# A retention + mixture-of-experts kernel: first loads issued from two queues, one weight quarter fetched and split later, the last result scaled by two engines

## Chip, cores and metric

The kernel runs on one core of a Trainium2 chip. The metric is the device time of one execution in microseconds (us). Several executions are timed, and their median is quoted.

## What is computed

The reference has two parts. The first is a linear attention with a decay for each head (batch 4, 8 heads, 768 positions, head size 64):

```python
for t in range(S):
    state = gamma[None, :, None, None] * state + np.einsum('bhd,bhe->bhde', k[:, :, t], v[:, :, t])
    y[:, :, t] = scale * np.einsum('bhd,bhde->bhe', q[:, :, t], state)
```

Its output, 3072 rows of 512 features, goes into a mixture of 8 experts. Each row is sent to the one expert with the largest logit:

```python
logits = x @ w_gate
expert_idx = np.argmax(logits, axis=1)
gate_w = probs[np.arange(N), expert_idx]
for e in range(E):
    mask = expert_idx == e
    h = np.maximum(x[mask] @ w1[e], 0.0)
    out[mask] = gate_w[mask, None] * (h @ w2[e])
```

## The kernel before, in words

The attention is done in 24 chunks of 128 positions, six for each batch entry. One chunk's inputs (q and k transposed, v and k as they are, 256 KB each) lie in one tile `qkv_t`, and five such tiles take turns (`AHEAD = 5`). `load(g)` (line 212) issues the transfer of chunk g on the queue of SyncE (SP); the first two chunks are loaded in halves, q and k first, then v and k. Of the last chunk of a batch entry the second k isn't loaded.

The order of the work is written out by hand; each engine executes its instructions in that order. The loop over chunks begins at line 440. Iteration g does, in this order: the scores of chunk g + 1 (`scores`, two PSUM tiles that VectorE multiplies by the mask M into `Sb`, line 239), `carry(g)` (the state's part of the output, line 266), `scale(g + 2)` (GpSimd weighs v into `vs`, line 225), one `split` if the table `SPLITS` names the iteration, the gate's logits in some iterations (line 310, their copy by ScalarE at line 312, transposes at line 321 and a reduction by VectorE at line 326), `update(g)` (the state, line 250, copied with a factor by ScalarE, line 255), `output(g)` (line 277, then VectorE's multiplication into `xT`, line 283), `rows(g - 1)` (transposes at line 291, ScalarE's copy at line 293), `load(g + 5)`, and a `fetch` if the table `fetches` names the iteration. Around chunk 1 the scores stand in other places (`LATE`). In the sixth chunk of a batch entry there is no `update`.

The weights of expert 0 are prepared during the attention. `fetch(0, part)` (line 124) loads one quarter of 1 MB into one of two tiles `raw`; `split(0, part, i, ...)` takes a quarter of that tile, rounds it with ScalarE into `whi` (line 132) and lets VectorE subtract that into `wlo` (line 133). `fetches` = {2: 0, 7: 1, 14: 2, 18: 3} says after which chunk each quarter is fetched, `SPLITS` in which iteration each of the 16 pieces is split (pieces 0 to 7 in iterations 6 to 13, pieces 8 to 13 in 18 to 23).

Ahead of the loop stand the first loads, the constants (`cs`, in two transfers, of which the first holds what M is built from; G; the gate's weights `wgs`; `us32`), `WARM = 16` matmuls on a tile of ones that give TensorE something to do until data arrive (line 416), and the building of M by VectorE (line 429).

After the attention the experts follow one another: hidden layer (line 786), relu and rounding (lines 791 and 792), output layer (lines 811 and 813). The last expert's result has three row blocks of 128, 128 and 104 rows. `put_rows` (line 721) has VectorE multiply each block in PSUM by the gate weight into `yo` (line 725), and GpSimd scatters its rows to the output (line 603).

Of the kernel before, what the change touches and what calls it, by code (L numbers as in the profile page):

```python
# [13 lines left out]
AF = mybir.ActivationFunctionType  # L14
ALU = mybir.AluOpType
# [5 lines left out]
P = 128  # L21
# [10 lines left out]
E1 = E - 1  # L32
E9 = E + 1
KD = DM // P
# [5 lines left out]
JMAX = -(-CMAX // 32)  # L40
IDS = 0x3FFF
FILLED = (160, 320)
WARM = 16
LATE = 0
FILL = (2, 2, 4, 2)
AHEAD = 5
# [2 lines left out]
GROUPS = ((0, 6), (6, 6), (12, 6), (18, 4), (22, 2))  # L49
SENDS = {**{g: (g - 8, g - 7) for g in range(8, 15)}, 15: (7, 9), 16: (9, 10), 17: (10, 12),  # L50
         **{g: (g - 8, g - 7) for g in range(20, 24)}}
SPLITS = {**{g: (g - 6,) for g in range(6, 14)}, **{g: (g - 10,) for g in range(18, 24)}}

OFF = {}
_n = 0
# [44 lines left out]
def retention_moe(ctx, tc, qkv, wg, wts, cst, gdec, ustr, out):  # L100
    nc = tc.nc
# [25 lines left out]
    def split(pos, part, i, engine, n=2):  # L127
        if i == 0:
            wparts[pos, part] = [wp.tile([P, 4, 512], F32R, name=n, tag="w", bufs=11) for n in ("whi", "wlo")]
        raw, (hi, lo) = raws[pos, part], wparts[pos, part]  # L130
        h = slice(n * i, n * i + n)
        nc.scalar.copy(out=hi[:, h], in_=raw[:, h])  # L132
        engine.tensor_tensor(out=lo[:, h], in0=raw[:, h], in1=hi[:, h].bitcast(F32), op=ALU.subtract)  # L133
# [52 lines left out]
    with ExitStack() as actx:  # L186
# [12 lines left out]
        G = flat[:, 0:NP * C].rearrange("p (n t) -> p n t", n=NP)  # L199
# [7 lines left out]
        qs, vss, Sbs, xTs, lgs, Ys = {}, {}, {}, {}, {}, {}  # L207
        state = {"half": 0, "low": 0}

        half = (slice(0, D), slice(D, P))  # L210

        def load(g, part=slice(0, 4)):
            if g not in qs:
                qs[g] = ld.tile([P, 4, DM], F32, name="qkv_t", tag="ld")
            nc.sync.dma_start(out=qs[g][:, part], in_=qkv[g][:, part])

        def turned(g, i):
            return qs[g][:, i].rearrange("a (p t) -> a p t", p=NP)

        def scale(g):  # L220
            c = g % CPB
            if c == CPB - 1:
                return
            vs = wk.tile([P, H, D], F32, name="vs", bufs=3)
            nc.gpsimd.tensor_tensor(  # L225
                out=vs, in0=qs[g][:, 2].rearrange("a (h d) -> a h d", d=D),
                in1=cv[:, c, :].unsqueeze(2).broadcast_to([P, H, D]), op=ALU.mult)
            vss[g] = vs.rearrange("a (n t) d -> a n (t d)", t=2)

        def scores(g):  # L230
            Sb = wk.tile([P, 2, NP, C], F32, name="Sb")
            q, kt = turned(g, 0), turned(g, 1)
            sps = [ps_s.tile([P, NP, C], F32, name="sp") for _ in range(2)]
            for p in range(NP):
                for r in range(2):
                    nc.tensor.matmul(out=sps[r][:, p, :], lhsT=kt[half[r], p, :], rhs=q[half[r], p, :],  # L236
                                     start=True, stop=True)
            for r in range(2):
                nc.vector.tensor_tensor(out=Sb[:, r], in0=sps[r], in1=M[:, r], op=ALU.mult)  # L239
            Sbs[g] = Sb  # L240
# [162 lines left out]
        def lows(n, engine):  # L403
            for f in range(state["low"], n):
                low(f, engine)
            state["low"] = n

        load(0, slice(0, 2))
        nc.sync.dma_start(out=cs[:, 0:NFIRST], in_=cst[:, 0:NFIRST])
        load(0, slice(2, 4))  # L410
        load(1, slice(0, 2))
        nc.sync.dma_start(out=G, in_=gdec)
        load(1, slice(2, 4))
        warm = ps_m.tile([P, 512], F32, name="warm", tag="mt")
        for i in range(WARM):
            nc.tensor.matmul(out=warm, lhsT=ones, rhs=ones.unsqueeze(1).broadcast_to([P, 4, P]),
# [3 lines left out]
        nc.vector.memset(wgs, 0.0)  # L420
        nc.vector.memset(zeros, 0.0)
        us32 = rawp.tile([P, P], F32, name="us32", tag="raw")
        nc.sync.dma_start(out=cs[:, NFIRST:], in_=cst[:, NFIRST:])
        nc.sync.dma_start(out=wgs[:, :, 0:E], in_=wg.rearrange("(k p) e -> p k e", p=P))
        for g in range(2, AHEAD):
            load(g)
        nc.sync.dma_start(out=us32, in_=ustr)
        for r in range(2):
            nc.vector.tensor_tensor(
                out=M[:, r], in0=causal.unsqueeze(1).broadcast_to([P, NP, C]), op=ALU.mult,  # L430
                in1=cv[:, 0].rearrange("a (n t) -> a t n", t=2)[:, r].unsqueeze(2).broadcast_to([P, NP, C]))
        scale(0)
        scores(0)
        scale(1)
        stages = []
        logits_at = {3: 0, **{2 * i + 2: i for i in range(1, NCH // 2 - 1)}}
        fetches = {2: 0, 7: 1, 14: 2, 18: 3}
        fills = {3: (slice(0, E9, E), slice(FILLED[0], EARLY)),
                 **{i + 3: (slice(2 * i - 1, min(2 * i + 1, E)), slice(FILLED[1], 32 * JMAX)) for i in range(1, 5)}}
        for g in range(NCH):  # L440
# [5 lines left out]
            if g + 2 < NCH:  # L446
                scale(g + 2)
            for i in SPLITS.get(g, ()):
                split(0, *divmod(i, 4), nc.vector, 1)
# [71 lines left out]
        for g in range(GROUPS[-1][0], NCH):  # L521
# [7 lines left out]
                                       op0=ALU.mult, op1=ALU.add)  # L529
# [64 lines left out]
def sliced(a):  # L594
    return a.rearrange("p (q k r) -> p k q r", q=4, k=KD)


def featured(a):
    return a.rearrange("p (k q r) -> p k q r", q=4, k=KD)


def scatter_rows(tc, out, index, rows, group="rows"):
    sc = tc.nc.gpsimd.indirect_dma_start(  # L603
        out=out, out_offset=bass.IndirectOffsetOnAxis(ap=index, axis=0),
        in_=rows, in_offset=None, bounds_check=out.shape[0] - 1, oob_is_err=False)
    tc.declare_no_dep(sc.ins, group=group, reason="every token has one slot: the scattered rows are disjoint")
    tc.add_to_no_dep_group(group, sc.ins)
# [68 lines left out]
def moe_main(ctx, tc, wparts, fetch, split, xhl1, xgs, load_x, load_meta, token_index, regions, beyond, limit, natural,  # L676
             overflow, out):
    nc = tc.nc
# [9 lines left out]
    widths = [[min(P, c - a) for a in range(0, c, P)] for c in CAPS]  # L688
# [32 lines left out]
    def put_rows(e, py, j):  # L721
        w = widths[e][j]
        index, weight = natural[e]
        yo = yp.tile([P, DM], F32, name="yo")
        nc.vector.tensor_scalar(out=sliced(yo[:w, :]), in0=featured(py[:w, :]), scalar1=weight[:w, j, 1:2],
                                scalar2=None, op0=ALU.mult)
        scatter_rows(tc, out, index[:w, j:j + 1], yo[:w, :])

    def turn(e, py, k):
# [13 lines left out]
    with tc.manual_schedule():  # L743
        for e in range(E):
# [52 lines left out]
            for k in range(steps):  # L797
# [4 lines left out]
                py = pys[k % 2]  # L802
                n = 0
                for f in range(KF):
                    whi, wlo = wparts[e, 2 + f // 4]
                    hh, hl = hs[f]
                    for a, x in ((whi, hh), (wlo, hh), (whi, hl)):
                        se = dict(start=(n == 0), stop=(n == 3 * KF - 1))
                        if e in natural:
                            w = widths[e][k]  # L810
# [5 lines left out]
                if e in natural:  # L816
                    put_rows(e, py, k)
                else:
                    turn(e, py, k)
# [147 lines left out]
```

## Time and profile before

| | |
|---|---|
| median of 3 runs | 408.57 us (408.56 to 409.14) |
| the profiled execution, its own time | 408.45 us |
| its span in the profile | 406.6 us |
| TensorE (PE) busy | 395.6 us, 97% |
| VectorE (DVE) busy | 251.8 us, 62% |
| ScalarE (ACT) busy | 154.0 us, 38% |
| GpSimd (POOL) busy | 157.6 us, 39% |
| moved by DMA | 81.48 MB, mean 200 GB/s |

The span is what the profiler saw; the execution's own time has 1.85 us around it. All times below are us from the start of the span. A matmul counts as busy until its modelled end, so a busy PE is not a PE at its peak; whether PE waited is told by the wait that stands behind an instruction, in brackets: how long the engine was idle before it, and what ended that. A wait for a DMA ends when the transfer has landed.

### The profile page before, as it was taken

What the parts mean: (1) busy time and instruction counts of PE and PEld (TensorE: products, weight loads), DVE (VectorE), ACT (ScalarE), POOL (GpSimd) and SP (SyncE); (2) the same over time, 40 slices, a digit from 0 to 9 for tenths busy, and PEclk for the clock granted to TensorE, in tenths of its full rate; (3) what the DMA queues carried; (4) which work ended last, traced back from release to release, by engine and by line L of the source; (5) the groups of instructions that cost most, each with busy time, mean ns of one, the idle gap of its engine ahead of it and who ended that gap; (6) DMA issues with size and microseconds to landing.
All of it is one profiled execution on the core that took longest, in us unless ns stands there. A gap on an engine that the chain in (4) does not pass through costs nothing. (4 is left out here: it accounts for less than half of the span.)

```text
span 406.6 us, 8299 instructions
## 1 busy us (share of the span) xinstructions
PE 395.6 (97%) x3279; PEld 359.6 (88%) x3279; DVE 251.8 (62%) x466; ACT 154.0 (38%) x306; POOL 157.6 (39%) x146
## 2 busy tenths in 40 slices
PE   8799989999999999999999999999999999999994
PEld 4678868787898989999999999999999999999972
DVE  3557778588664576574677396557829557675410
ACT  2243535355651543440453154235325324523200
POOL 1322183723780031000178048308704831850741
PEclk9999999999999999999999999999999999999999
DMA  8999999996439694555158335906733682530111
GB/s 278 414 350 381 407 406 345 350 409 193 160 137 231 200 252 148 195 161 144 42 207 225 112 129 183 272 5 235 216 123 123 220 229 61 192 137 2 49 52 45
DMA packets 31177, 81.48 MB, mean 200 GB/s; under 512 B 5146, under 2 KB 19614, under 8 KB 24736
## 3 DMA queue, kind: packets, MB, share of 16 engines
q1 hardware_dynamic: 26096, 68.24, 50.2%
q0 software_dynamic: 5040, 12.69, 8.8%
q8 instruction: 26, 0.43, 0.4%
q14 instruction: 15, 0.12, 0.1%
HBM read 65.50 MB, written 16.15 MB: 201 GB/s over the span
## 5 line engine op out<-in xcount | busy, mean ns | idle before, releaser
L603 POOL DMA_INDIRECT out<-Z,sidx x80 | 93.8, 1173 | 140.3 <-DVE Z L738 119.0
L133 DVE TENSOR_TENSOR wlo<-raw,whi 128x1024 fp32r<-128x1024 f32 (+1 forms) x72 | 82.1, 1142 | 16.4 <-ACT whi L132 16.1
L132 ACT CAST whi<-raw 128x1024 fp32r<-128x1024 f32 (+1 forms) x72 | 68.1, 949 | 3.0 <-DMA raw<-w 2.9
L791 ACT ACTIVATE hh<-ph 128x256 fp32r<-128x256 f32 (+7 forms) x64 | 31.5, 492 | 97.0 <-PE ph L786 96.5
L813 PE MATMUL py<-hl,whi 128*128 128x452 f32 (+5 forms) x192 | 66.9, 349 | 0.0
L813 PE MATMUL py<-hh,whi 128*128 128x452 f32 (+5 forms) x192 | 66.9, 348 | 0.0
L813 PE MATMUL py<-hh,wlo 128*128 128x452 f32 (+5 forms) x192 | 66.9, 348 | 0.0
L792 DVE SCALAR_TENSOR_TENSOR hl<-ph,hh 128x256 fp32r<-128x256 f32 (+7 forms) x64 | 35.6, 556 | 36.5 <-ACT hh L791 35.4
L786 PE MATMUL ph<-xh,wlo 128*128 128x452 f32 (+6 forms) x224 | 50.1, 345 | 0.0
L786 PE MATMUL ph<-xl,whi 128*128 128x452 f32 (+6 forms) x224 | 50.0, 345 | 0.0
L786 PE MATMUL ph<-xh,whi 128*128 128x452 f32 (+6 forms) x224 | 49.9, 345 | 0.0
L239 DVE TENSOR_TENSOR Sb<-sp,xgs 128x512 f32<-128x512 f32 x48 | 30.9, 685 | 17.7 <-PE sp L236 17.6
L786 PEld LDWEIGHTS ph<-xh,whi 128*128 128x128 f32 x224 | 40.7, 188 | 0.9
L786 PEld LDWEIGHTS ph<-xh,wlo 128*128 128x128 f32 x224 | 40.7, 188 | 0.7
L786 PEld LDWEIGHTS ph<-xl,whi 128*128 128x128 f32 x224 | 40.5, 188 | 0.7
L225 POOL TENSOR_TENSOR vs<-qkv_t,cs 128x512 f32<-128x512 f32 x20 | 20.9, 1045 | 44.2 <-DMA qkv_t<-qkv 38.8
L622 ACT CAST xh<-xt 128x512 fp32r<-128x512 f32 (+7 forms) x26 | 14.3, 555 | 60.7 <-DVE xt L613 60.7
L813 PEld LDWEIGHTS py<-hl,whi 128*128 128x128 f32 x192 | 36.1, 188 | 0.8
L813 PEld LDWEIGHTS py<-hh,wlo 128*128 128x128 f32 x192 | 36.1, 188 | 0.8
L813 PEld LDWEIGHTS py<-hh,whi 128*128 128x128 f32 x192 | 36.1, 188 | 0.7
L603 POOL DMA_INDIRECT xs_dram<-xn,KEY x24 | 24.8, 1033 | 22.2 <-DVE Sb L239 8.5
L733 DVE STREAM_TRANSPOSE Z<-py 128x416 f32<-128x416 f32 (+3 forms) x24 | 15.0, 627 | 27.3 <-PE py L813 27.2
(120 smaller groups left out, 530.9 us busy)
## 6 DMA issues: line engine op xcount, KB each, us to landing
raw<-w SPq DMA_DIRECT2D x32, 1024.0 KB, 5.2
qkv_t<-qkv SPq DMA_DIRECT2D x18, 1024.0 KB, 9.2
qkv_t<-qkv SPq DMA_DIRECT2D x4, 768.0 KB, 9.0
xgs<-xs_dram SPq DMA_DIRECT2D x12, 211.2 KB, 7.6
xs_dram<-xn SPq DMA_DIRECT2D x7, 325.0 KB, 9.9
qkv_t<-qkv SPq DMA_DIRECT2D x4, 512.0 KB, 4.8
xgs<-xs_dram SPq DMA_DIRECT2D x8, 195.0 KB, 7.0
out<-Z,sidx POOLq DMA_INDIRECT x80, 4.3
```

What stands on the lines that cost most here:

```text
L132: nc.scalar.copy(out=hi[:, h], in_=raw[:, h])
L133: engine.tensor_tensor(out=lo[:, h], in0=raw[:, h], in1=hi[:, h].bitcast(F32), op=ALU.subtract)
L225: nc.gpsimd.tensor_tensor(out=vs, in0=qs[g][:, 2].rearrange("a (h d) -> a h d", d=D), in1=cv[:, c, :].unsqueeze(2).broadcast_to([P, H, D]) ...
L239: nc.vector.tensor_tensor(out=Sb[:, r], in0=sps[r], in1=M[:, r], op=ALU.mult)
L603: sc = tc.nc.gpsimd.indirect_dma_start(out=out, out_offset=bass.IndirectOffsetOnAxis(ap=index, axis=0), in_=rows, in_offset=None, bounds_c ...
L622: nc.scalar.copy(out=xh[:, :, sl], in_=src)
L733: nc.vector.transpose(out=Zs[e][:, 0:nb, k, :], in_=py[:, 0:32 * nb].rearrange("p (j c) -> p j c", c=32))
L786: nc.tensor.matmul(out=ph[:, :cap], lhsT=wparts[e, f // 4][a][:, kd, fo:fo + P], rhs=x[:, kd, :cap], start=(n == 0), stop=(n == 3 * KD - 1))
L791: nc.scalar.activation(out=hh[:, :cap], in_=ph[:, :cap], func=AF.Relu)
L792: nc.vector.scalar_tensor_tensor(out=hl[:, :cap], in0=ph[:, :cap], scalar=0.0, in1=hh[:, :cap].bitcast(F32), op0=ALU.max, op1=ALU.subtract)
L813: nc.tensor.matmul(out=py[:, :cap], lhsT=a[:, f % 4, k * P:(k + 1) * P], rhs=x[:, :cap], **se)
```

## The change

Four things: the halves of the first two chunks are each loaded in two transfers of 64 partitions, one issued by SP and one by ScalarE, with the other early transfers in another order; the dummy matmuls go from 16 to 9 and chunk 0's `vs` is made by VectorE; the second weight quarter is fetched after chunk 9 instead of 7, and its four pieces are split in iterations 13 to 16 instead of 10 to 13; the last row block is scaled in two halves of 256 columns, one by VectorE and one by ScalarE.

```diff
-WARM = 16
+WARM = 9
...
-SPLITS = {**{g: (g - 6,) for g in range(6, 14)}, **{g: (g - 10,) for g in range(18, 24)}}
+SPLITS = {**{g: (g - 6,) for g in range(6, 10)}, **{g: (g - 9,) for g in range(13, 17)}, **{g: (g - 10,) for g in range(18, 24)}}
...
-        def load(g, part=slice(0, 4)):
+        def load(g, part=slice(0, 4), apart=False):
             if g not in qs:
                 qs[g] = ld.tile([P, 4, DM], F32, name="qkv_t", tag="ld")
-            nc.sync.dma_start(out=qs[g][:, part], in_=qkv[g][:, part])
+            for queue, rows in zip((nc.sync, nc.scalar), half) if apart else ((nc.sync, slice(0, P)),):
+                queue.dma_start(out=qs[g][rows, part], in_=qkv[g][rows, part])
...
-        def scale(g):
+        def scale(g, engine=nc.gpsimd):
...
-            nc.gpsimd.tensor_tensor(
+            engine.tensor_tensor(
...
-        load(0, slice(0, 2))
+        load(0, slice(0, 2), True)
         nc.sync.dma_start(out=cs[:, 0:NFIRST], in_=cst[:, 0:NFIRST])
-        load(0, slice(2, 4))
-        load(1, slice(0, 2))
-        nc.sync.dma_start(out=G, in_=gdec)
-        load(1, slice(2, 4))
+        load(0, slice(2, 4), True)
+        nc.scalar.dma_start(out=G, in_=gdec)
+        load(1, slice(0, 2), True)
+        load(1, slice(2, 4), True)
...
+        load(2)
         nc.sync.dma_start(out=cs[:, NFIRST:], in_=cst[:, NFIRST:])
+        load(3)
         nc.sync.dma_start(out=wgs[:, :, 0:E], in_=wg.rearrange("(k p) e -> p k e", p=P))
-        for g in range(2, AHEAD):
-            load(g)
         nc.sync.dma_start(out=us32, in_=ustr)
+        load(4)
...
-        scale(0)
+        scale(0, nc.vector)
...
-        fetches = {2: 0, 7: 1, 14: 2, 18: 3}
+        fetches = {2: 0, 9: 1, 14: 2, 18: 3}
...
-        nc.vector.tensor_scalar(out=sliced(yo[:w, :]), in0=featured(py[:w, :]), scalar1=weight[:w, j, 1:2],
-                                scalar2=None, op0=ALU.mult)
+        first = KD // 2 if e == E1 and j == len(widths[e]) - 1 else KD
+        to, turned, share = sliced(yo[:w, :]), featured(py[:w, :]), weight[:w, j, 1:2]
+        nc.vector.tensor_scalar(out=to[:, 0:first], in0=turned[:, 0:first], scalar1=share, scalar2=None, op0=ALU.mult)
+        if first < KD:
+            nc.scalar.activation(out=to[:, first:], in_=turned[:, first:], func=AF.Copy, scale=share)
```

What this does to the order of the instructions on an engine, at three places. A row is a line number, the operation, the tile written and the tiles read; in brackets stand the semaphores that it waits for. DMAHW0 to DMAHW7 are eight semaphores that the transfers issued by SP and ScalarE take in turn, so the ninth transfer of the program waits until the first has landed.

The first place is SP's queue at the start of the program, before and then with the change:

```order
L215 DMA qkv_t<-qkv 128x1024
L409 DMA cs<-cst 128x200
L215 DMA qkv_t<-qkv 128x1024 x2
L412 DMA xgs<-gdec 128x512
L215 DMA qkv_t<-qkv 128x1024
L423 DMA cs<-cst 128x373
L424 DMA xgs<-wg 128x4x8 [waits DVE_49]
L215 DMA qkv_t<-qkv 128x2048 [waits DMAHW0_49]
L215 DMA qkv_t<-qkv 128x2048 [waits DMAHW1_49]
L215 DMA qkv_t<-qkv 128x2048 [waits DMAHW2_49]
L427 DMA us_149<-ustr 128x128 [waits DMAHW3_49]
```

```order
L216 DMA qkv_t<-qkv 64x1024
L410 DMA cs<-cst 128x200
L216 DMA qkv_t<-qkv 64x1024 x2
L216 DMA qkv_t<-qkv 64x1024 [waits DMAHW0_49]
L216 DMA qkv_t<-qkv 128x2048 [waits DMAHW2_49]
L425 DMA cs<-cst 128x373 [waits DMAHW3_49]
L216 DMA qkv_t<-qkv 128x2048 [waits DMAHW4_49]
L427 DMA xgs<-wg 128x4x8 [waits DMAHW5_49,DVE_49]
L428 DMA us_146<-ustr 128x128 [waits DMAHW6_49]
L216 DMA qkv_t<-qkv 128x2048 [waits DMAHW7_49]
```

The rows of 128x2048 are chunks 2, 3 and 4. Chunk 2 now stands ahead of the second part of the constants and the gate's weights, chunk 3 ahead of the gate's weights, and chunk 4 behind `us32`; G is gone to ScalarE's queue. Chunk 2 now waits for a half of chunk 0's v (DMAHW2) where it waited for chunk 0's q and k.

The second place is ScalarE in iterations 10 and 11, the first that lose a split, before, and then in iterations 10 to 13 with the change:

```order
L132 CAST whi<-raw 128x512 [waits DMAHW6_49]
L312 COPY xgs<-L 128x256 [waits PE_49,Activation_49]
L255 ACTIVATE ub_118<-U,cs 128x64 [waits PE_49]
L255 ACTIVATE ub_118<-U,cs 128x64 x3
L293 COPY xn<-xp 128x4x128 [waits PE_49]
L132 CAST whi<-raw 128x512
```

```order
L313 COPY xgs<-L 128x256 [waits PE_49,Activation_49]
L256 ACTIVATE ub_118<-U,cs 128x64 [waits PE_49]
L256 ACTIVATE ub_118<-U,cs 128x64 x3
L294 COPY xn<-xp 128x4x128 [waits PE_49]
L294 COPY xn<-xp 128x4x128 [waits DMAHW4_49,DMAHW5_49,DMAHW3_49,DMAHW6_49,DMAHW1_49,DMAHW7_49,DMAHW0_49,PE_49]
L313 COPY xgs<-L 128x256 [waits PE_49,Activation_49]
L256 ACTIVATE ub_117<-U,cs 128x64 [waits PE_49]
L256 ACTIVATE ub_117<-U,cs 128x64 x3
L294 COPY xn<-xp 128x4x128 [waits PE_49]
L358 ACTIVATE ex<-sh 128x48 [waits DVE_49]
L132 CAST whi<-raw 128x512 [waits DMAHW4_49]
```

The rounding that waits for the fetched quarter stood ahead of iteration 10's copy of the logits; it is now behind the exponential that ends iteration 12.

The third place is the end of the program, VectorE's row and then ScalarE's and GpSimd's, with the change:

```order
L729 TENSOR_SCALAR yo<-py_2072,meta_2076 104x2x4x32 [waits DMASW4_49,DVE_49,PE_49]
```

```order
L731 ACTIVATE yo<-py_2072,meta_2076 104x2x4x32 [waits DMASW4_49,DMAHW6_49,DMASW2_49,DVE_49]
```

```order
L605 DMA out<-yo,sidx_2077 3072x512 [waits DMASW6_49,Activation_49]
```

Before there was one row of 104x4x4x32 on VectorE, and the scatter waited for VectorE. The product on ScalarE waits for VectorE and not for PE, though it reads what PE wrote; the scatter waits for ScalarE.

## Rows read from the trace of the kernel before

**Rows 1.** The page's head and the DMA line of its second part: the span, and the busy share of the DMA engines in 40 equal slices of it, in tenths.

```profile
span 406.6 us, 8299 instructions
...
DMA  8999999996439694555158335906733682530111
```

**Rows 2.** All waits of PE in the program, the two largest of those that lie behind the first instruction: who waited for whom, us in total, times, the longest.

```profile
PE sp L236 <- DMA qkv_t<-qkv: 2.1, 2, 1.2
...
PE Y L266 <- DVE lg L326: 0.9, 1, 0.9
```

**Rows 3.** The timeline of PE during the attention: start, duration, engine, line, operation, tiles, count, and in brackets the idle time before and its releaser. The rows of L236 are the scores with which iterations begin: those at 6.67 and 13.59 are chunks 0 and 2, that at 17.31 is chunk 3 and begins iteration 2; those at 25.64, 30.19 and 33.49 begin iterations 4, 5 and 6, those at 49.70, 54.63 and 58.90 iterations 10, 11 and 12.

```profile
1.08 5.66 PE L416 MATMUL warm<-ones 128*128 128x512 bf16 x16 [1.08 <-DVE ones L143]
6.67 1.16 PE L236 MATMUL sp<-qkv_t 64*128 64x128 f32 x16
...
13.59 1.16 PE L236 MATMUL sp<-qkv_t 64*128 64x128 f32 x16 [1.20 <-DMA qkv_t<-qkv]
...
17.31 1.16 PE L236 MATMUL sp<-qkv_t 64*128 64x128 f32 x16 [0.95 <-DMA qkv_t<-qkv]
...
25.64 1.16 PE L236 MATMUL sp<-qkv_t 64*128 64x128 f32 x16
...
30.19 1.16 PE L236 MATMUL sp<-qkv_t 64*128 64x128 f32 x16
...
33.49 1.16 PE L236 MATMUL sp<-qkv_t 64*128 64x128 f32 x16
...
49.70 1.16 PE L236 MATMUL sp<-qkv_t 64*128 64x128 f32 x16
...
54.63 1.16 PE L236 MATMUL sp<-qkv_t 64*128 64x128 f32 x16
56.69 0.67 PE L266 MATMUL Y<-qkv_t,ub 64*64 64x128 f32 x16 [0.90 <-DVE lg L326]
...
58.90 1.16 PE L236 MATMUL sp<-qkv_t 64*128 64x128 f32 x16
```

**Rows 4.** The timeline of ScalarE and VectorE around the second quarter: its first rounding, the copy of the logits behind it and the subtraction; and, in the last line, the rounding with which iteration 13 began.

```profile
53.32 0.62 ACT L132 CAST whi<-raw 128x512 fp32r<-128x512 f32 x1 [2.92 <-DMA raw<-w]
53.84 0.37 ACT L312 COPY xgs<-L 128x256 f32<-128x256 f32 x1
...
53.97 1.98 DVE L133 TENSOR_TENSOR wlo<-raw,whi 128x512 fp32r<-128x512 f32 x1 [1.79 <-ACT whi L132]
...
65.11 0.60 ACT L132 CAST whi<-raw 128x512 fp32r<-128x512 f32 x1
```

**Rows 5.** SP's timeline: the issue of the gate's weights, of the second quarter, and of chunks 13 and 14, ahead of which the quarter stood (SP's rows have the time it took to issue, not to land).

```profile
4.34 0.45 SPq L424 DMA_DIRECT2D xgs<-wg  x1
...
42.26 0.34 SPq L124 DMA_DIRECT2D raw<-w  x1
45.27 4.32 SPq L215 DMA_DIRECT2D qkv_t<-qkv  x2
```

**Rows 6.** The timeline of VectorE and GpSimd at the start: M, chunk 0's v and chunk 1's v weighed as they land, and chunk 0's masked scores.

```profile
5.16 1.29 DVE L429 TENSOR_TENSOR xgs<-cs 128x512 f32<-128x512 f32 x2 [3.06 <-DMA cs<-cst]
...
6.58 1.04 POOL L225 TENSOR_TENSOR vs<-qkv_t,cs 128x512 f32<-128x512 f32 x1 [6.11 <-DMA qkv_t<-qkv]
...
7.87 1.29 DVE L239 TENSOR_TENSOR Sb<-sp,xgs 128x512 f32<-128x512 f32 x2 [1.42 <-PE sp L236]
...
10.26 1.04 POOL L225 TENSOR_TENSOR vs<-qkv_t,cs 128x512 f32<-128x512 f32 x1 [2.64 <-DMA qkv_t<-qkv]
```

**Rows 7.** The page's part on DMA issues: the gate's weights, with the time from issue to landing.

```profile
xgs<-wg SPq DMA_DIRECT2D x1, 16.0 KB, 6.7
```

**Rows 8.** Stretches of half a microsecond at the start, and of two microseconds later: us, PE, PEld, DVE, ACT and POOL busy, PE's granted clock, the busy share of the DMA engines, GB/s.

```profile
1.50:2.00 0.50, 0.50 (x3) 0.22 (x2) 0.50 (x1) 0.50 (x1) 0.00 (x0) 1.00 0.36 98
2.00:2.50 0.50, 0.50 (x3) 0.20 (x2) 0.10 (x1) 0.23 (x2) 0.00 (x0) 1.00 0.50 164
...
11.00:11.50 0.50, 0.50 (x18) 0.39 (x16) 0.29 (x1) 0.00 (x0) 0.30 (x1) 1.00 1.02 426
...
70.00:72.00 2.00, 2.00 (x28) 1.66 (x26) 1.48 (x7) 1.33 (x5) 0.23 (x1) 1.00 0.67 242
72.00:74.00 2.00, 2.00 (x50) 1.71 (x50) 1.29 (x2) 0.14 (x1) 1.70 (x2) 1.00 0.81 311
```

**Rows 9.** The timeline of PE's weight loads at the end of the dummy matmuls, one load to each matmul.

```profile
4.90 0.15 PEld L416 LDWEIGHTS <-ones 128*128 128x128 bf16 x1 [0.28 <-issue]
...
5.29 0.96 PEld L416 LDWEIGHTS <-ones 128*128 128x128 bf16 x5 [0.24 <-issue]
```

**Rows 10.** The timeline at the end of the program: VectorE's last product and GpSimd's last scatter.

```profile
400.95 0.75 DVE L725 TENSOR_SCALAR yo<-py,meta 104x512 f32<-104x512 f32 x1 [4.81 <-PE py L811]
402.01 1.01 POOL L603 DMA_INDIRECT out<-yo,sidx  x1 [4.62 <-DVE yo L725]
```

**Rows 11.** Groups of instructions from 100 to 145 us, by shape, two that read 256 columns of PSUM: count, busy us, mean ns of one, idle before.

```profile
L792 DVE SCALAR_TENSOR_TENSOR hl<-ph,hh 128x256 fp32r<-128x256 f32 x8 | 3.4, 422 | 3.0 <-ACT hh L791 3.0
L649 ACT ACTIVATE rx<-ph 128x256 f32<-128x256 f32 x8 | 3.1, 383 | 5.1 <-PE ph L645 4.3 <-POOL hl L653 0.8
```

**Rows 12.** The timeline late in the attention: chunk 20 lands, which GpSimd waits for, and PE begins with its scores.

```profile
85.21 1.04 POOL L225 TENSOR_TENSOR vs<-qkv_t,cs 128x512 f32<-128x512 f32 x1 [3.22 <-DMA qkv_t<-qkv]
...
86.96 1.16 PE L236 MATMUL sp<-qkv_t 64*128 64x128 f32 x16
```

## The prediction

> **What bounds the kernel now.** I first read PE's row of waits, because PE is busy for nearly the whole span of 406.6 us [rows 1]. Behind its first instruction the list has only two waits of weight: 2.1 us in two pieces for `qkv_t`, that is, for input chunks to land, and 0.9 us once for VectorE [rows 2]. So the kernel goes at PE's pace, and what can be gained lies at those waits, at PE's own work, and at the tail behind PE's last matmul.
>
> The timeline of PE says where the waits are: 1.20 us ahead of chunk 2's scores at 13.59, 0.95 us ahead of chunk 3's at 17.31, and 0.90 us in iteration 11 at 56.69 [rows 3]. From 17.31 on PE runs without a wait for data to iteration 10. So whatever moves the row at 17.31 moves everything behind it, and what shortens PE's way ahead of that row only makes it wait longer there.
>
> The DMA engines are the second thing to look at: through the first quarter of the span their share is nearly full [rows 1]. PE and DMA are close to each other in the attention, so a PE that runs ahead may find its chunks not landed. That is taken up below.
>
> The sum is made against the profiled execution, 408.45 us, which is 0.12 under the median of 408.57; I add that back at the end.
>
> **The second quarter, fetched and split later.** Iteration 10 lasts 54.63 - 49.70 = 4.93 us. Iteration 4 has the same place in its batch entry and the same work on PE, and lasts 30.19 - 25.64 = 4.55. Iteration 11 lasts 58.90 - 54.63 = 4.27, iteration 5 with the same work 33.49 - 30.19 = 3.30 [rows 3]. So 0.38 + 0.97 = 1.35 us are lost there. The reason is a queue: the quarter's transfer is issued at 42.26 [rows 5] and ScalarE stands for 2.92 us until 53.32 for it, with the copy of the logits behind it (53.84); VectorE begins its subtraction at 53.97 and takes 1.98 [rows 4], and what stands behind that on VectorE is the reduction that PE's row at 56.69 waits for. The change has no split in iterations 10 to 12, and ScalarE's copy of the logits there waits for PE alone. I take the whole 1.35.
>
> Does the wait come back in iteration 13? The fetch now stands behind chunk 14's transfer, issued by 49.6 [rows 5]; with the 53.32 - 42.26 = 11.1 us that the quarter took before it lands at about 60.7, less what PE gains. The rounding of iteration 13 ran at 65.11 [rows 4], behind iteration 12's exponential, and will be some 1.9 earlier, at 63.2. So 2.5 us are in hand; the transfer would have to take 13.6 us. The pieces themselves are 0.6 us of ScalarE [rows 4] and about 0.65 of VectorE (M's two products over 512 columns take 1.29 [rows 6]) in iterations of 3.3 to 4.6 us; up to 1.98 on VectorE has been seen [rows 4]. I cost them at nothing, hidden behind PE. Chunks 13 and 14 lose a megabyte ahead of them, which costs nothing either.
>
> **The start.** What counts is when chunk 3 lands. Two things change that.
>
> Order: ahead of chunk 3 only the gate's weights go away; the second part of the constants still stands between chunks 2 and 3. Chunk 1's v landed at 10.26 [rows 6], the gate's weights at 4.34 + 6.7 = 11.04 [rows 5, 7]. Of these 0.78 us the constants (128 x 373 x 4 B = 0.19 MB) need 0.45 at the 426 GB/s of a full stretch [rows 8]. That leaves 0.33 for the weights, the gain by order.
>
> Two queues: from 1.5 to 2.5 us the DMA engines are at 0.36 and 0.50 of their time [rows 8]; 0.57 us are idle. If that is SP's issuing, a second queue gives up to 0.57; if it is the latency of a first transfer, nothing; a loss of as much as the order brings, 0.33, is conceivable, since halves on two queues interleave and chunk 0 may land later. I take the middle of nothing and 0.57, about 0.3. Together 0.6: chunk 3 at 16.7.
>
> [...]
>
> The upper end: from chunk 2 to chunk 3 3.72 us pass (13.59 to 17.31, [rows 3]), where a chunk's 1.05 MB needs 2.46 at 426 GB/s. If the 1.26 us between are not lost again, the start gives 0.6 + 1.26 = 1.86.
>
> PE is no bound before that. Without its two waits it would reach chunk 3 at 17.31 - 1.20 - 0.95 = 15.16 [rows 3]. Now the dummy matmuls, 0.15 + 0.28 = 0.43 us apart [rows 9], end at 1.08 + 9 x 0.43 = 4.95, and the scores begin there, not at 6.67. But VectorE then builds M until 6.45, weighs chunk 0's v when it has landed (6.58) in about 0.65, and begins with the masked scores at 7.25 rather than 7.87 [rows 6]. So PE's way gets 0.6 shorter, to about 14.5, some 2.2 ahead of chunk 3. The fewer dummies and VectorE's product are thus costed at nothing; the wait for chunk 3 covers them. SP's issue of chunk 2 now waits for half of chunk 0's v, at about 6.6; then chunk 1 and G, 1.3 MB or 3 us of DMA work, are still ahead of it, so no gap opens.
>
> **The end.** The two halves are not at once: by the order ScalarE's product waits for VectorE's. VectorE's half takes 0.42 and ScalarE's 0.38 [rows 11], the handover 0.03 (53.94 to 53.97, [rows 4]): 0.83 in place of 0.75 [rows 10]. I take 0.1 longer. At once it would be 0.42, 0.33 shorter; and with a ScalarE that takes 0.62, as for 512 columns [rows 4], 0.3 longer.
>
> [...]
>
> **Does it stay gained?** Chunk 20 lands at 85.21 and is wanted at 86.96 [rows 12], 1.75 us in hand, and PE will come 1.95 earlier. But its transfer is issued when PE frees a buffer and so moves too, and the DMA engines had idle time in front of it: 0.66 and 0.38 us from 70 to 74 [rows 8]. So it can land 1.04 earlier, and 0.8 stay in hand. If it didn't move at all, 0.2 would be given back. Behind the attention no wait of PE is listed that reaches 0.9 [rows 2].
>
> **Sum:** -1.35 - 0.6 + 0.1 = -1.85; 408.45 becomes 406.6, and against the median **406.7 us**. Its own range is 406.3 to 407.1.
>
> **The rivals.**
> - *The queues bring nothing.* The start gives 0.33 by order or less: 408.57 - 1.35 - 0.33 + 0.1 = 407.0, with nothing at all from the start 407.3. For it: half the early idle may be latency. Chance 0.20. [...]
> - *Chunk 3 comes without its delay.* 408.57 - 1.35 - 1.86 + 0.1 = 405.5. For it: the delay between chunks 2 and 3 has no cause in the order of transfers; against: the same engines and nearly the same bytes. Chance 0.15.
> - *The stall moves.* The quarter lands after 63.2 or VectorE is too full in iterations 13 to 16, and 1.35 come back: 408.57 - 0.6 + 0.1 = 408.1. Against: 2.5 us in hand. Chance 0.12.
> - *Slower: PE stays at its lower clock.* [...] Chance 0.04.
>
> **How the numbers follow.** The forecast has 0.46, 0.03 are left to other things. 0.2% is 0.82 us, about what a measurement can tell from no change, so the line is at 407.75. The forecast and the first two rivals lie below it, 0.81, with a little of the rest: 0.82 faster. The moved stall lies within 0.2%: 0.13 with what is left. Slower: 0.05. The range takes in the first two rivals with the ends of their unknowns, 405.2 to 407.6; it leaves out the moved stall and the lower clock, and a start or end worse than any bound.
>
> **What would show it.** Right: chunk 3's scores at 16.4 to 17.0 and still with a wait for `qkv_t` ahead of them; iterations 10 and 11 at about 4.55 and 3.30 with no wait of ScalarE for `raw`; ScalarE's last product beginning when VectorE's ends. Wrong: a wait of PE for VectorE or of ScalarE for `raw` in iterations 13 to 16; waits for `qkv_t` at chunks 20 or 21; scores of 2.3 us in the first 15 us; the scatter at the end earlier, against PE's last matmul, than now.

## The result: 411.62 us, slower by 0.6%, and the profile after

The changed kernel takes 411.62 us (median of 6 runs, 410.29 to 412.01), the kernel before, beside it, 408.85 (6 runs, 408.56 to 409.83). The ratio is 1.0059, 95% interval 1.0041 to 1.0077: 2.4 us slower, where 406.7 was forecast. The profiled execution has 410.98, its span is 2.5 longer than in [rows 1].

From the page of the changed kernel, its span and the clock granted to PE in 40 slices of about 10 us:

```profile
span 409.1 us, 8294 instructions
...
PEclk9799999999999999999999999999999999999999
```

The timeline of PE in the changed kernel answers to [rows 3]. The rows at 5.03, 13.74, 17.88 and 20.98 are the scores of chunks 0 to 3, those at 53.37, 57.93 and 61.23 begin iterations 10, 11 and 12:

```profile
1.08 4.02 PE L417 MATMUL warm<-ones 128*128 128x512 bf16 x9 [1.08 <-DVE ones L143]
5.03 1.72 PE L237 MATMUL sp<-qkv_t 64*128 64x128 f32 x16
10.99 1.12 PE L251 MATMUL U<-vs,qkv_t 128*64 128x64 f32 x16 [4.24 <-DVE vs L226]
...
13.74 2.29 PE L237 MATMUL sp<-qkv_t 64*128 64x128 f32 x16
...
17.88 1.16 PE L237 MATMUL sp<-qkv_t 64*128 64x128 f32 x16 [0.50 <-DMA qkv_t<-qkv]
...
20.98 1.16 PE L237 MATMUL sp<-qkv_t 64*128 64x128 f32 x16 [0.33 <-DVE xT L284]
...
53.37 1.16 PE L237 MATMUL sp<-qkv_t 64*128 64x128 f32 x16
...
57.93 1.16 PE L237 MATMUL sp<-qkv_t 64*128 64x128 f32 x16
...
61.23 1.16 PE L237 MATMUL sp<-qkv_t 64*128 64x128 f32 x16
```

Three differences to [rows 3] make the whole result. Chunk 3's scores begin at 20.98 and not at 17.31: 3.67 us lost before anything else happens, and iteration 10 begins those 3.67 later (53.37, 49.70). Iterations 10 and 11 then last 4.56 and 3.30 instead of 4.93 and 4.27, so at iteration 12 the loss is 2.33. The last is at the end of the program. In time order, PE's last matmul and what follows, the answer to [rows 10]:

```profile
402.82 0.40 PE L816 MATMUL py<-whi,hl 128*104 128x512 f32 x1
403.26 0.48 DVE L729 TENSOR_SCALAR yo<-py,meta 104x256 f32<-104x256 f32 x1 [4.81 <-PE py L816]
403.78 0.47 ACT L731 ACTIVATE yo<-py,meta 104x256 f32<-104x256 f32 x1 [16.73 <-DVE yo L729]
404.56 1.02 POOL L605 DMA_INDIRECT out<-yo,sidx  x1 [4.86 <-DVEq L592]
```

PE's last matmul in the kernel before:

```profile
400.51 0.40 PE L811 MATMUL py<-whi,hl 128*104 128x512 f32 x1
```

The product on ScalarE begins where VectorE's ends. From the start of PE's last matmul to the scatter 1.74 us pass, where it was 1.50 (400.51 to 402.01 in the kernel before). So 3.67 - 1.34 + 0.24 = 2.57, less 0.02 between iteration 12 and PE's last matmul (2.31 later than before): the 2.5 of the span. What is to be explained is the start.

Stretches of five microseconds at the start, changed kernel, columns as in [rows 8]:

```profile
5.00:10.00 5.00, 1.75 (x17) 1.40 (x16) 1.29 (x2) 1.44 (x2) 0.00 (x0) 0.88 1.00 240
10.00:15.00 5.00, 4.01 (x40) 3.62 (x42) 2.58 (x4) 0.93 (x4) 0.00 (x0) 0.50 1.04 253
15.00:20.00 5.00, 4.44 (x77) 3.67 (x74) 2.25 (x4) 0.93 (x4) 2.09 (x2) 0.94 1.06 394
```

The same stretches of the kernel before:

```profile
5.00:10.00 5.00, 4.68 (x56) 2.88 (x54) 2.58 (x4) 0.93 (x4) 1.04 (x1) 1.00 1.01 371
10.00:15.00 5.00, 3.80 (x72) 3.26 (x72) 2.23 (x4) 0.93 (x4) 2.08 (x2) 1.00 1.04 422
```

The last two columns tell it: the DMA engines are as busy as before (1.00 and 1.04 of their time) and move 240 and 253 GB/s instead of 371 and 422. They aren't idle and don't wait for an issue; each byte takes them longer. Until about 15 us, while the halves are in flight, 10 us at some 150 GB/s less are 1.5 MB, or 3.5 us at 426. A share of 1.04 stood beside 253 GB/s here and beside 422 before, so the share alone doesn't tell the rate. PE's clock (third column from the end) falls to 0.50 behind PE's wait of 4.24 for chunk 0's v, and the scores at 13.74 take 2.29, where those at 17.88, with the clock back at 1.00, take 1.16.

### The profile page after: what moved, and what is told of

Read it like the earlier page. It is cut to its first block, busy times and chain, and to the rows that moved or that the text cites. A ratio compares the mean times of both kernels' runs of the same rounds, so it can differ in the third digit from the quotient of the medians.

```text
span 409.1 us, 8294 instructions
## 1 busy us (share of the span) xinstructions
PE 396.3 (97%) x3272; PEld 361.4 (88%) x3272; DVE 252.1 (62%) x467; ACT 154.8 (38%) x307; POOL 156.3 (38%) x145
## 3 DMA queue, kind: packets, MB, share of 16 engines
q0 software_dynamic: 5040, 12.69, 8.7%
## 5 line engine op out<-in xcount | busy, mean ns | idle before, releaser
L226 POOL TENSOR_TENSOR vs<-qkv_t,cs 128x512 f32<-128x512 f32 x19 | 19.9, 1047 | 47.7 <-DMA qkv_t<-qkv 38.9
```

The costliest lines, as they stand in the source:

```text
L226: engine.tensor_tensor(out=vs, in0=qs[g][:, 2].rearrange("a (h d) -> a h d", d=D), in1=cv[:, c, :].unsqueeze(2).broadcast_to([P, H, D]), o ...
```

## Experiments

Four readings of the slow start. **A**: a transfer into 64 adjoining partitions costs the DMA engines more time for each byte, by whichever queue. **B**: two queues at once hinder each other. **C**: PE's lower clock makes the start late. **D**: the new order of loads, where chunk 2's issue waits for a half of chunk 0's v. The runs were taken later, in sessions in which the kernel before itself had a median of 416.75 to 418.26 us, with a wait of PE of 2.7 to 4.2 us around 110 us in every trace, and behind it another 302 to 308 us that don't follow what was changed at the start (300 in the traces of the kernel before and of the changed kernel, which are from the first session). Totals are therefore given as ratios to the kernel before beside them, and the argument goes by the first 20 us of the traces. In these sessions the kernels with the old loads had chunk 3's scores at 17.54 to 18.25, so a few tenths between two single traces mean nothing.

### Is it the halves, the queues or the clock?

**Both halves on SP.**

```diff
-zip((nc.sync, nc.scalar), half)
+zip((nc.sync, nc.sync), half)
```

> The changed kernel with both halves of each early load issued by SP; ScalarE's queue keeps G alone. Theory A (a transfer into 64 adjoining partitions keeps the DMA engines busy longer for its bytes, whatever the queue): still slow, chunk 0's v lands at 9 to 12 us, the DMA engines move about 240 GB/s at a full share until chunks 0 and 1 are in, about 411 us or more. Theory B (two queues at work on the same engines slow each other): chunk 0's v lands at 6.5 to 7, about 400 GB/s from 5 us on, 407.0 to 407.8 us.

Ratio 1.0054 (1.0009 to 1.0099). Its stretch from 5 to 10 us:

```profile
5.00:10.00 5.00, 2.02 (x22) 1.63 (x24) 2.41 (x4) 0.00 (x0) 0.00 (x0) 0.81 1.06 238
```

Chunk 3's scores begin at 20.50 behind a wait of 1.83 for their data. One queue is as slow as two (238 and 240 GB/s).

**Two queues that carry whole tensors** of 128 partitions (SP q and v, ScalarE k and the second k).

```diff
+pieces = [(nc.sync, slice(part.start, part.start + 1)), (nc.scalar, slice(part.start + 1, part.stop))]
```

> The changed kernel with each early load divided by tensor instead of by partition: SP loads q and v, ScalarE k and the second k, all 128 partitions in each transfer. As many transfers, queues and semaphores as in the changed kernel. Theory A: fast, chunk 0's v at 6.5 to 7.2 us, 407.0 to 407.8 us. Theory B: slow as the changed kernel, v at about 10 us, about 411 us.

Ratio 0.9944 (0.9904 to 0.9983). Its stretch from 5 to 10 us:

```profile
5.00:10.00 5.00, 3.21 (x41) 2.67 (x42) 3.18 (x5) 2.29 (x6) 0.00 (x0) 0.98 1.04 381
```

From 10 to 15 us it moves 410 GB/s; chunk 3's scores begin at 17.21 without a wait for data. B is out.

**Even and odd partitions** in place of the lower and upper half, again 64 rows on each queue.

```diff
-zip((nc.sync, nc.scalar), half)
+zip((nc.sync, nc.scalar), (slice(0, P, 2), slice(1, P, 2)))
```

> The changed kernel with the halves taken as even and odd partitions: still 64 partitions to a transfer, two queues, the same sizes and order, but each transfer reaches over all 128. Theory A in its form that adjoining partitions are the trouble: fast, v at 6.5 to 7.2 us, 407.0 to 407.8 us. Theory A in the form that 64 rows to a transfer are the trouble, and theory B: slow, v at about 10 us, about 411 us.

Ratio 1.0021 (0.9977 to 1.0064), 367 GB/s from 5 to 10 us, chunk 3's scores at 18.13 without a wait for data. ScalarE's queue from 4.5 to 14 us (packets, MB, share of 16 engines' time), first in the changed kernel:

```profile
q10 hardware_dynamic: 387, 1.05, 48.3%
```

and with even and odd partitions:

```profile
q10 hardware_dynamic: 390, 1.04, 28.8%
```

Nearly the same packets and bytes take 1.7 times as long when the 64 rows adjoin. Neither the number of rows nor of packets nor of queues differs.

**PE kept busy** by twenty more dummy matmuls behind chunk 0's scores.

```diff
         scores(0)
+        for i in range(20):
+            nc.tensor.matmul(out=warm, lhsT=ones, ...)
```

> The changed kernel with 20 more dummy matmuls behind chunk 0's scores, so that PE is busy while it waits for chunk 0's v. Theory C (the lower clock of PE from 8.7 to 15.6 us, after its wait of 4.2 us, is what makes the start late): PE runs at its higher clock from 6 us on, chunk 3's scores come 1 to 3 us earlier than 20.98 and the time falls to 408.5 to 410.5 us. Theories A and B: the clock rises but chunk 3's scores stay at 20.5 to 21.1, since the chunk lands at 20.8, and the time stays within 0.5 us of 411.4.

Ratio 1.0070 (1.0022 to 1.0118). The stretches:

```profile
5.00:10.00 5.00, 4.35 (x30) 2.46 (x31) 1.60 (x3) 1.46 (x2) 0.00 (x0) 1.00 1.01 223
10.00:15.00 5.00, 4.78 (x70) 3.38 (x68) 2.94 (x6) 0.93 (x4) 0.00 (x0) 1.00 1.06 228
```

The clock is at 1.00 up to 15 us and the rate no better; chunk 3's v is at hand at 21.88 and its scores begin at 21.91. The lower clock is a consequence, not the cause.

**The halves alone** in the kernel before, the rest as it was.

```diff
-load(0, slice(0, 2))
+load(0, slice(0, 2), True)
...
```

> The kernel before with nothing but its first two chunks' halves each loaded as two transfers of 64 adjoining partitions, one by SP and one by ScalarE. Theory A: 230 to 250 GB/s at a full share of the DMA engines from 5 to 13 us, chunk 3's scores 3 to 4 us later than the kernel before, at 20.3 to 21.3, ratio about 1.008 to 1.009. If the change's other order of loads has a part in its loss (rival D: chunk 2's issue behind a half of chunk 0's v): chunk 3's scores at 17.3 to 18.5, ratio 1.000 to 1.003.

Ratio 1.0108 (1.0047 to 1.0169). 255 GB/s from 5 to 10 us; chunk 3 lands at 21.07, and its scores, with PE's clock at 0.50 from 17.5 to 20 us, begin at 22.42, later than expected. Without the new order chunk 3 comes as late (20.84 in the changed kernel), so D is out too.

**Another cut**: ScalarE's queue carries partitions 32 to 95, again 64 adjoining rows, SP's the outer two times 32.

```diff
+pieces = [(nc.sync, slice(0, 32)), (nc.sync, slice(96, P)), (nc.scalar, slice(32, 96))]
```

> The change with the rows of each early load cut in another way: ScalarE's queue carries partitions 32 to 95, again 64 adjoining rows in one transfer, SP's the outer 0 to 31 and 96 to 127. It tells apart two readings of theory A. If 64 adjoining rows as such are slow, ScalarE's queue needs as long for its 1.05 MB from 4.5 to 14 us as in the changed kernel (48% of the 16 engines' time there), and the rate stays at 230 to 250 GB/s. If what counts is which partitions are reached, ScalarE's queue needs 28 to 36% for them, and the rate from 5 to 12.5 us is 280 to 380 GB/s, between the halves and the interleaved rows; chunk 3's scores at 18 to 19.5 us. [...]

Its stretch from 5 to 10 us:

```profile
5.00:10.00 5.00, 1.67 (x17) 1.45 (x16) 1.29 (x2) 0.37 (x2) 0.00 (x0) 0.95 1.01 296
```

and ScalarE's queue from 4.5 to 14 us:

```profile
q10 hardware_dynamic: 329, 0.84, 29.6%
```

29.6% of 16 engines' 9.5 us for 0.84 MB are 54 us of an engine for each MB; the changed kernel has 70 and the even and odd rows 42 by the same division. So 64 adjoining rows as such aren't the cause: moved by 32 they are served faster. What each cut changes is both the partitions that a transfer writes and the rows of the chip's memory that it reads, and no run separates the two. Chunk 3's scores at 19.85 are later than expected: its data had landed by 17.52, and PE's clock was 0.50 from 10 to 15 us. The ratio, 1.0119 (1.0073 to 1.0165), is more than a start 1.1 us ahead of the changed kernel's would give; that rest isn't explained.

From 5 to 10 us the rates are 223 to 255 GB/s with halves, 367 with even and odd rows and 296 with the third cut. What in the way of the bytes makes them so isn't shown.

### The other parts of the start

**Whole loads, else as changed** (nine dummies, new order, G on ScalarE's queue), and **the same with sixteen dummies and the last product undivided**.

```diff
-zip((nc.sync, nc.scalar), half) if apart else ((nc.sync, slice(0, P)),)
+((nc.sync, slice(0, P)),)
```

```diff
-WARM = 9
+WARM = 16
...
-first = KD // 2 if e == E1 and j == len(widths[e]) - 1 else KD
+first = KD
```

> The change with every early load as one transfer of 128 partitions on SP; everything else of the change stays. Theory A (a transfer into 64 adjoining partitions costs the rate): the DMA engines move 370 to 420 GB/s from 5 to 15 us, chunk 0's v is weighed at about 6.6 to 7.2, chunk 3's scores begin at 16.8 to 17.5, and against the kernel before the whole is -1.35 (second quarter) + 0.24 (tail) - 0 to 0.5 (start) = -1.1 to -1.6 us, a ratio of about 0.9965. Rival C' (what is left of the change at the start, nine dummy matmuls, the other order, VectorE's product, is slow by itself, through the lower clock): chunk 3's scores at 19 or later though its data lie there, ratio 1.000 or more.

> The same with each early load as one transfer of 128 partitions on SP (G alone on ScalarE's queue). It prices the second queue where no half is involved. Theory A: the queue is worth little, chunk 3's scores within 0.3 us of the kernel with tensors on two queues, 16.5 to 17.0 us, ratio 0.995 to 0.996. If the two queues are worth what the prediction bounded (0.57 us): chunk 3's scores 0.5 to 0.6 us later than there.

Ratios 0.9994 (0.9960 to 1.0027) and 0.9998 (0.9956 to 1.0040), both less gain than expected and with intervals too wide to tell. The starts differ. Chunk 3's scores with nine dummies, then with sixteen:

```profile
17.77 1.16 PE L237 MATMUL sp<-qkv_t 64*128 64x128 f32 x16
...
16.00 1.16 PE L237 MATMUL sp<-qkv_t 64*128 64x128 f32 x16 [0.33 <-DVE xT L284]
```

With nine, chunk 3's v is at hand at 16.74 and its scores begin a microsecond later, PE's clock at 0.50 to 0.62 from 7.5 to 15 us; with sixteen the clock stays at 1.00.

**The same pair with tensors on two queues**, the last product undivided.

> The change with two queues that each carry whole tensors of 128 partitions (SP q and v, ScalarE k and the second k), and VectorE alone for the last product, as before. Theory A: rate 410 GB/s from 7.5 to 15 us, chunk 3's scores at about 17.2 without a wait for its data, the end from PE's last matmul to the scatter 1.10 us as before, so -1.35 - 0.1 + 0 = about -1.5 us or a little more, ratio 0.996; 0.24 us under the same kernel with the split tail. Theory B (two queues hinder each other): chunk 3's scores at 20 or later, ratio 1.003 or more.

> Two queues with whole tensors of 128 partitions, VectorE alone for the last product, and sixteen dummy matmuls as before in place of nine. Theory: with nine, PE's wait for chunk 0's v and the clock at 0.5 behind it eat what the order of loads wins (chunk 3 has landed by 16.5 us, PE comes for it at 16.9 to 17.2). With sixteen the clock stays at 1.00 up to chunk 3, whose scores then begin when it lands, at 16.2 to 16.7 us: -0.6 to -1.1 against the kernel before's 17.3, and -1.35 from the second quarter, in all about -2.1 us, ratio 0.995. Rival: the clock does not matter there, chunk 3's scores at 16.9 to 17.3 as with nine, -1.35 to -1.7 us, ratio 0.9963.

Ratios 0.9978 (0.9947 to 1.0010) and 0.9998 (0.9965 to 1.0030). With nine chunk 3's scores begin at 16.86, with sixteen at 17.52 behind a wait of 1.60 for data. That the data came a microsecond later than with nine wasn't expected. The rate isn't the reason (408 and 413 GB/s from 10 to 15 us): Chunks 2 and 3 have 256 packets of 8 KB, but 364 of that size or more had been started by 17.52, so chunk 4's went ahead of chunk 3's last. Why they did so in this run isn't known. What the pair shows is that a second queue has no gain over 16.00 of the whole loads on one.

**Order alone**, **nine dummies with VectorE's v alone** (both in the kernel before), and **sixteen dummies in the changed kernel**.

```diff
-load(1, slice(0, 2))
-nc.sync.dma_start(out=G, in_=gdec)
+nc.scalar.dma_start(out=G, in_=gdec)
+load(1, slice(0, 2))
...
+load(2)
 nc.sync.dma_start(out=cs[:, NFIRST:], in_=cst[:, NFIRST:])
+load(3)
...
-for g in range(2, AHEAD):
-    load(g)
 nc.sync.dma_start(out=us32, in_=ustr)
+load(4)
```

> The kernel before with the change's order of loads alone, each a whole transfer on SP, G on ScalarE's queue: chunks 2 and 3 ahead of the second part of the constants and of the gate's weights. Forecast's reading: chunk 3's scores 0.33 us earlier than the kernel before, at 17.0 (17.3 to 18.2 in kernels with the old order). Rival, from the kernel with whole loads and sixteen dummies: 1.3 us or more earlier, at 16.0 to 16.4, since the gate's weights are 1024 pieces of 32 bytes that hold the DMA engines far longer than their 16 KB.

> The kernel before with nine dummy matmuls and chunk 0's v weighed by VectorE, nothing else. Forecast's reading: the wait for chunk 3 covers it, chunk 3's scores at 17.3 to 18.2 as in kernels with the old loads, waiting for their data. Rival: PE waits 1.5 to 2.2 us for chunk 0's v, its clock falls to 0.50 for some us, and chunk 3's scores come without a wait for data, 0.5 to 1.5 us later than in the kernel before.

> The change with sixteen dummy matmuls in place of nine. If the halves alone make the loss and the lower clock is their consequence: the rate at 230 to 250 GB/s as in the change, chunk 3's scores when it lands, at 20.5 to 21.5 us with a wait for data, ratio 1.004 to 1.008 as the change. If the dummies have a part in it: chunk 3's scores at 19 or earlier, ratio 1.002 or less.

Ratios 1.0008 (0.9967 to 1.0048), 1.0022 (0.9981 to 1.0063) and 1.0159 (1.0088 to 1.0230). Chunk 3's scores with the order alone:

```profile
16.01 1.16 PE L236 MATMUL sp<-qkv_t 64*128 64x128 f32 x16 [0.42 <-DMA qkv_t<-qkv]
```

with nine dummies and VectorE's v alone:

```profile
18.12 1.16 PE L236 MATMUL sp<-qkv_t 64*128 64x128 f32 x16
```

and in the changed kernel with sixteen:

```profile
21.09 1.16 PE L237 MATMUL sp<-qkv_t 64*128 64x128 f32 x16 [0.79 <-DMA qkv_t<-qkv]
```

The order alone brings 1.3 us at this point, four times the forecast, though its total doesn't show it. Three kernels with whole loads in the new order and sixteen dummies have 15.93 to 16.01, three traces with the old order and sixteen 17.31 to 18.25; tensors on two queues with sixteen, at 17.52, are the exception. The expectation's rival named the packets of the gate's weights as the reason. There are 512 of them, of 32 bytes (not 1024), and the trace has 9 ns for each, so 0.29 us of the 16 engines in all. Nor does the rate decide. What the DMA engines had moved from 0 to 16.01 us, in the kernel before:

```profile
DMA packets 1883, 5.27 MB, mean 329 GB/s; under 512 B 671, under 2 KB 927, under 8 KB 1567
```

and with the order alone:

```profile
DMA packets 2021, 5.27 MB, mean 329 GB/s; under 512 B 688, under 2 KB 1072, under 8 KB 1712
```

The bytes are the same, but chunk 3 is there in the second and lands at 17.18 in the first. Chunk 3 and all that stands ahead of it are 4.77 MB, so half a megabyte of what stands behind it, mostly chunk 4, had been moved by then, and in the kernel before 0.97 by 17.18. The order's gain is that fewer of chunk 4's packets go ahead of chunk 3's last ones. The records don't tell the 16 engines apart, so why they get that far ahead isn't shown.

Sixteen dummies don't help the changed kernel: the halves still hold chunk 3 until 21, 5.1 us behind the order alone. So the start's account reads 17.3 - 1.3 (order) + 5.1 (halves) = 21.1, and the nine dummies are covered there. With whole loads they aren't: chunk 3's scores come 1.8 later with nine (17.77 and 16.00), 1.0 of it behind data that lay there.

### The quarter, the tail, and both good parts together

**The second quarter alone.**

```diff
-range(6, 14)}, ...
+range(6, 10)}, **{g: (g - 9,) for g in range(13, 17)}, ...
-fetches = {2: 0, 7: 1,
+fetches = {2: 0, 9: 1,
```

> The kernel before with the second quarter fetched after chunk 9 and split in iterations 13 to 16, nothing else. All theories: iterations 10 and 11 last 4.55 and 3.30 us in place of 4.93 and 4.27, no wait in iterations 13 to 16, -1.35 us, ratio 0.9967. If the stall moves: ratio 0.999 to 1.000 and a new wait of PE behind iteration 12.

Ratio 0.9991 (0.9962 to 1.0020). The total can't tell 1.35 us there; the trace can. Iterations 10, 11 and the start of 12:

```profile
49.94 1.16 PE L236 MATMUL sp<-qkv_t 64*128 64x128 f32 x16
...
54.49 1.16 PE L236 MATMUL sp<-qkv_t 64*128 64x128 f32 x16
...
57.79 1.16 PE L236 MATMUL sp<-qkv_t 64*128 64x128 f32 x16
```

They last 4.55 and 3.30, as in the changed kernel. Against the expectation two short waits of PE follow in iterations 15 and 16, 0.36 us for VectorE at 71.79 and 0.32 for ScalarE at 77.08; the changed kernel's trace has none there.

**The last product in two halves alone**, in the kernel before.

> The kernel before with only the last product split between VectorE and ScalarE. In series: from PE's last matmul to the scatter 1.34 us in place of 1.10, ScalarE's product beginning where VectorE's ends; +0.24 us, ratio 1.0006. At once: 0.4 us shorter, ratio 0.999.

Ratio 1.0042 (0.9999 to 1.0085); VectorE's half at 415.15, ScalarE's at 415.67, the scatter at 416.45, 1.74 behind the start of PE's last matmul. In series, +0.24 against 1.50.

**Order and quarter**, whole loads on SP, sixteen dummies, GpSimd's v and the undivided tail: what was worth keeping.

> The kernel before with the change's order of loads (whole, on SP, G on ScalarE's queue) and the second quarter's move, nothing else. Expected from the parts: -1.35 from the quarter, -0.3 (forecast's order) to -1.3 (rival's), in all -1.7 to -2.7 us, ratio 0.9935 to 0.996; iterations 10 and 11 at 4.55 and 3.30 us; chunk 3's scores at 16.0 to 17.0.

Ratio 0.9943 (0.9907 to 0.9978), so this one was faster than the kernel before beside it. The whole loads with sixteen dummies above differ from it only in that VectorE makes chunk 0's `vs`; they have the same start (16.00) and gave 0.9998 (0.9956 to 1.0040) in another session. The two intervals overlap, so the gain is shown by one of two nearly equal kernels. Chunk 3's scores:

```profile
15.93 1.16 PE L236 MATMUL sp<-qkv_t 64*128 64x128 f32 x16 [0.31 <-DVE xT L283]
```

Iteration 10 lasts 4.55; iteration 11 lasts 4.20, with a wait of 0.82 for VectorE's reduction, so with PE ahead by 1.3 us some of the old stall is back. Why VectorE is late there wasn't tried.

## Why the prediction was wrong

- **What bounds the kernel** was right: all 3.67 us by which chunk 3 came later stood in the row of iteration 10 unchanged.
- **The second quarter** was right to 0.01: 4.56 and 3.30, and it didn't come back. In the changed kernel the copy of the logits in iteration 10 waits for PE alone, and the first rounding of iteration 13 waits for nothing:

```profile
55.82 0.37 ACT L313 COPY xgs<-L 128x256 f32<-128x256 f32 x1 [1.75 <-PE L L311]
...
67.86 0.60 ACT L132 CAST whi<-raw 128x512 fp32r<-128x512 f32 x1
```

- **The start, order**: right in direction, 0.33 forecast and about 1.3 measured. The weights themselves were priced about right (their packets took 0.29). What I left out is the rest of the queue: chunk 4 stands directly behind chunk 3 in the old order, and its packets go ahead of chunk 3's last. From chunk 2's v to chunk 3's (GpSimd's products) 3.81 us pass in the kernel before, 13.53 to 17.34, and 3.34 with the order alone, 12.69 to 16.03, though the constants, 0.45, now stand between the two. So 0.9 of the 1.26 us are gone that the rival *Chunk 3 comes without its delay* had and for which I saw no cause in the order.
- **The start, two queues**: this is the step that failed. It took 0.3 as a gain, between 0.57 and a loss of 0.33. Measured is a loss of about 5 us with the new order (21.09 and 16.01). The step treated a half as the same bytes on another queue; it bounded the queue and not the shape. No row of before has a load into 64 adjoining partitions, and the bound for a loss, "halves on two queues interleave", came from the order's gain instead of from what a lower rate would do: 2.1 MB of halves at half of 426 GB/s, 213, near the 223 to 255 that were measured, are 4.9 us more. The rival at 407.0 had no gain from the queues; the measurement is far on the other side of that.
- **Fewer dummies at nothing** held, but for a reason that spoils the lesson: chunk 3 came so late that anything was covered. Where chunk 3 can come at 16, its scores began up to 1.8 later with nine, more than the order gives.
- **The slower rival**, at 0.04: that PE would stay at a lower clock was an estimate of mine, and no run shows it low all the way from chunk 0's scores to chunk 3's. What the runs showed is a clock of 0.50 from about 9 to 15 us, behind a wait of 4.24 for data; with it held at 1.00 up to 15 us the start is as late (21.91). So the kernel is slower, but the cause is not PE's clock.
- **The tail**: in series as forecast; 0.24 and not 0.1, since the halves took 0.48 and 0.47 where I took 0.42 and 0.38 from 128 x 256 products of other kinds. ScalarE's wait for VectorE is in the program, so no run shows the two products at once.

## What to carry to other kernels

Cutting one load into two by partitions was not a free change of queue: from 5 to 10 us the lower and upper 64 rows ran at 223 to 255 GB/s, even and odd rows at 367, loads divided by tensor at 372 to 387 and whole loads in the same order at 399 to 421. So before such a cut, look at which rows each piece carries, and prefer cuts along the free axis or whole loads. Read the DMA engines' share and their GB/s together; a share of 1.00 at 240 GB/s, where 1.01 had stood beside 371, was the sign. And when a trace has no row of an operation's new shape, bound its rate as well as its issue, over all the bytes that change shape.

## What the runs showed of the hardware

- Loads into the lower and the upper 64 partitions, by one queue or two, ran at 223 to 255 GB/s from 5 to 10 us with the DMA engines full; whole loads in the new order at 399 to 421 (four kernels), even and odd rows at 367.
- By 16.01 us two orders of the same loads had moved the same 5.27 MB; a load was complete in one and 1.2 us short of it in the other, since packets of the load behind it had gone ahead. 512 packets of 32 bytes took 9 ns each, 0.29 us of the 16 engines.
- PE's clock fell to a mean of 0.50 over 2.5 us (0.61 in one trace) behind waits of PE for chunk 0's v of 1.46 to 4.24 us with nine dummies ahead (eight traces). With sixteen it stayed at 1.00 behind waits of 1.25, 1.63 and 1.78; behind one of 3.20 its mean was 0.70 from 10 to 12.5 us and 0.62 from 12.5 to 15.
